# Sliding-window attention into a gated feed-forward layer: chunks 4 to 9 as units of 512 columns, with probabilities, packed sinks and ranks held elsewhere

## The chip, the cores and the metric

The kernel runs on one core of one Trainium2 chip. The metric is the device time of one execution in microseconds (us), taken from several executions; the profile is of one further execution, with its own time.

## What is computed

The reference is attention with four sink tokens and a window of 128, followed by a feed-forward layer with the activation h * tanh(softplus(h)). There are 4 batches, 8 heads, 768 positions, head size 64; then 3072 tokens of width 512 and a hidden width of 2048.

```python
scores = np.matmul(q, k.transpose(0, 1, 3, 2)) / np.sqrt(D)
keep = is_sink | ((rel >= 0) & (rel < window))
a = exp(where(keep, scores, -1e9) - max); a = a / (sum(a) + 1e-09)
x = np.matmul(a, v).transpose(0, 2, 1, 3).reshape(B * S, H * D)
h = x @ w_in
g = h * np.tanh(log1p(exp(h)))
out = g @ w_out
```

Inputs of the attention are float32, the two weight matrices float64.

## The kernel before

The tokens are worked in 12 chunks of 256 (two row tiles of 128). Chunks 0 to 3 are the first of the four batches, which see no token before them; chunks 4 to 11 are the others, sorted by batch. For each chunk, attention is done for four pairs of heads (`pair`, then `outs`) and leaves x, transposed, as a high and a low part, each exact in the format that TensorE multiplies in one pass. The feed-forward layer takes its products three times: high by high, high by low and low by high. The hidden width is cut into 16 pieces `f` of 128, or 8 pairs of pieces `f2`.

*Three forms of the feed-forward layer.* Chunks 0 to 2 are worked in turns of two `f2` each, while the weights still arrive and are split by ScalarE, VectorE and GpSimd (`weights`): `step`, narrow, products of 256 columns (L584). Chunks 3 to 9 use `step`, wide: for each piece `f` there is a result block `hp` of 2 x 256 columns, and for each of the four pieces of the inner dimension a product of 512 columns, the high weights with x's high and low part side by side (L580), and one of 256 columns, the low weights with x's high part (L581):

```python
yield nc.tensor.matmul(hp.t, wih[f].t[:, fs], xt, start=kt == 0, stop=False)
yield nc.tensor.matmul(hp.t[:, 0, :], wil[f].t[:, fs], xt[:, 0, :], start=False, stop=kt == KT - 1)
```

VectorE adds the two halves of `hp` (TENSOR_REDUCE, L590) into a block `n`. The activation follows on ScalarE and VectorE for 512 numbers at once (Exp L593, min L594, Square L595, Ln L596, Exp L597, and the product with h L598), then the copy to the high part `gh` (in the helper, L271) and the low part `gl` (in the helper, L282 to L284). The second layer is 12 products of 512 columns into two accumulators `acc` (L614). Chunks 10 and 11 together use `double`: for each piece `f`, 12 products of 512 columns, the tokens of both chunks side by side (L642), into a block that is in turn a `hp` and an `att` block, with no reduction, then the activation (Exp L645, product L650) and 12 products (L668) into four accumulators, two of tag `att` and two of tag `acc`.

*What sets the order.* Every operation is a task with a rank and one or more engines that may run it. `Plan.solve` runs through them in time with a cost for each, takes the task that can start first and among those the one of lowest rank, and so fixes the order on each engine. Blocks of SBUF and PSUM are taken by tag in the numbers of the table `TAGS`: 81 of `w`, two each of `u`, `n`, `gh`, `p2`, `sk`; in PSUM four `att`, two `hp`, two `acc`. Ranks of the feed-forward steps count through `sequence`; ranks of the attention come from `att_rank`, by a formula for chunks 3 and up. Where a plan leaves TensorE without work for some time, `emit` puts products of zeros (L786, `ZERO` columns each) there. The instructions then wait for each other by semaphores alone, as the chip runs.

*The last tile's result* leaves in two halves, one from VectorE by the queue of SP and one from ScalarE by its own queue, out of one block `w` (`store`, L687 to L694).

Of the kernel before, what the change touches and what calls it, by code (L numbers as in the profile page):

```python
# [46 lines left out]
PEN_C, PEN_S, PEN_N, PEN_J, PEN_W = 147, 0, 239, 268, 58  # L47
OTP, OVP = 1.2, 1
OTF, OVF, PACE = 1.089, 0.601, 1.542
WA, WB, WO = 1.203, -1.766, 0.423  # L50
GROUP, PART, SPARED = 3, 2, 20
PITCHN = 7
LEAD, LEADG, LEADN = 11, (54.195, 35.033, 35.128), 9
WARM, AHEAD, COLD, SPARE, ROOM = 10, 5, 2500, 250, 4
ZERO = 224
SPL = 1.5
# [187 lines left out]
class Fast(Base):  # L244
# [108 lines left out]
    def halves(self, b, j0, i0, w, pr, rank):  # L353


        nc, add = self.nc, self.plan.add
        kr, ks = Buf("raw", [P, 512, 2], I32), [Buf("w", [P, w], F32R) for _ in range(2)]
        qr, qa, qb = Buf("w", [P, 2, T]), Buf("w", [P, 2, T], F32R), Buf("w", [P, 2, T], F32R)
# [11 lines left out]
        r = rank + SPL  # L370
        k = []
        for e, z in enumerate(ks):
            a = add(r, self.copy_ways(w, lambda z=z: z.t, lambda e=e: half()[:, e, :]), ldk, [kr], [z])
            k.append(add(r + .02, self.sub_ways(w, lambda z=z: z.t[low], lambda e=e: half()[low, e, :], lambda z=z: f32(z.t[low]), more=HALF), [a], [kr, z]))
        a = add(r + .01, self.copy_ways(2 * T, lambda: qa.t, lambda: qr.t), ldq, [qr], [qa])
        q = add(r + .03, self.sub_ways(2 * T, lambda: qb.t, lambda: qr.t, lambda: f32(qa.t)), [a], [qr, qa], [qb])
        return ks, (qa, qb), [*k, q]

    def pair(self, b, c3, pr, rank, x, sk, soft):
# [6 lines left out]
        p2 = Buf("p2", [P, 6 * P])  # L386
        last, norms, sums = [], [], []
        for i in range(TB):
            r = rank + i
# [31 lines left out]
            for e in range(2):  # L421
                new = ([p2] if i == 0 else []) + ([] if soft and i else [nm, sm]) if e == 0 else []
                old = [z for z in (p2, nm, sm) if z not in new]
                j = e + 2 * i * soft
                at_ = (2 * P * i if first else 2 * WM * i) + n * e
                pv = lambda at_=at_, n=n: p2.t[:, at_:at_ + n]
# [15 lines left out]
            for e in range(2 * (not soft)):  # L442
                at_ = (2 * P * i if first else 2 * WM * i) + n * e
                row = lambda at_=at_, n=n: p2.t[:, at_:at_ + n]
# [10 lines left out]
            def tr(pt=pt, cols=cols, i=i, n=n):  # L455
                for e in range(2):
                    for x in range(2):
                        if cols[x] is not None:
                            yield nc.tensor.transpose(pt.t[:, e, x * P:(x + 1) * P], p2.t[:, 2 * P * i + n * e + cols[x]:2 * P * i + n * e + cols[x] + P], self.ident)  # L459
# [5 lines left out]
        if not first:  # L465
            pt = Buf("att", [P, 2, TB, P])

            def tr():
                for i in range(TB):
                    for e in range(2):  # L470
                        yield nc.tensor.transpose(pt.t[:, e, i, :], p2.t[:, (2 * i + e) * WM + SK:(2 * i + e + 1) * WM], self.ident)  # L471
# [8 lines left out]
            for z in (up, low):  # L480
# [5 lines left out]
                                                              lambda: p2.t[:, 0:rows].rearrange("p (i e c) -> p e i c", i=TB, e=2)[:, :, :, 0:SK]),  # L486
# [10 lines left out]
    def outs(self, first, rank, parts, x_done, sk, soft):  # L497
# [15 lines left out]
        if not first:  # L513
            ssk = Buf("att", [P, P])
            a = add(rank + OTP + 1.02, {PE: (109, lambda: nc.tensor.transpose(ssk.t, sk.t, self.ident))}, self.packs, [sk], [ssk])
# [104 lines left out]
    def double(self, sts, f, rank, begins, ends, wdeps):  # L620
# [29 lines left out]
        e = add(r + .55, {DVE: (dve_t(N), lambda: nc.vector.scalar_tensor_tensor(m.t, u.t, 1.0, hp.t, ALU.subtract, ALU.mult))}, [a], [u, hp], [m])  # L650
        gg = add(r + .57, self.copy_ways(N, lambda: gh.t, lambda: m.t), [e], [m], [gh])
        final = f == NF - 1
# [9 lines left out]
        for k, (t, part) in enumerate(((0, 0), (1, 0), (0, 1), (1, 1), (2, 0), (2, 1), (3, 0), (3, 1)) if final else order):  # L662
# [8 lines left out]
            if done:  # L671
                self.store(st, r, t, final, 2 * TB - 1)

    def store(self, st, r, t, final, last=None):
# [10 lines left out]
        ot = Buf("w" if last else "u", [P, DM])  # L685
# [3 lines left out]
        elif t == last:  # L689
            for z, (e, dma) in enumerate(((DVE, nc.sync), (ACT, nc.scalar))):  # L690
                cs = slice(z * T, (z + 1) * T)
                a = add(r + 1.7 + .1 * t, self.copy_ways(T, lambda cs=cs: ot.t[:, cs], lambda cs=cs: acc.t[:, cs], True, (e,), -1.0),
                        [st.tail], [acc] + ([ot] if z else []), [] if z else [ot])
                add(r + 1.8 + .1 * t, {SP if z == 0 else ACT: (460, lambda cs=cs, dma=dma: dma.dma_start(self.out[st.row + t * P:st.row + (t + 1) * P, cs], ot.t[:, cs]), 2500)}, [a], [ot])  # L694
# [10 lines left out]
    def sequence(self, chunks):  # L705
# [6 lines left out]
        return seq + [(n, f2) for n in range(GROUP, chunks - 2) for f2 in range(NU)] + [(chunks - 2, f) for f in range(NF)]  # L712

    def run(self):
# [8 lines left out]
        for n, (b, c3) in enumerate(chunks):  # L723
            st = SimpleNamespace(row=b * S + c3 * T, x_done=[], part={})
            if n == len(chunks) - 1:
                st.x = states[-1].x
            else:
                st.x = [[Buf("w", [P, 2, T], F32R) for _ in range(1 + (n == len(chunks) - 2))] for _ in range(KT)]
            part = n - len(chunks) + 2
            held = []  # L730
            for pr in range(NPAIR):
                if not held:
                    sk = Buf("sk", [P, P])
# [213 lines left out]
def constants(nc, top, tmp, lim):  # L947
# [18 lines left out]
    c.older, c.newer, c.elder = t([P, P], F32, "older"), t([P, P], F32, "newer"), t([P, P], F32, "elder")  # L966
# [128 lines left out]
```

## Time and profile before

| what | value |
|---|---|
| median of 3 runs | 684.61 us (684.59 to 685.14) |
| the profiled execution's own time | 686.47 us |
| its span | 684.7 us |
| granted clock of TensorE | 0.997 |
| TensorE busy | 677.2 us, 99% |
| TensorE's weight loads busy | 573.4 us, 84% |
| VectorE busy | 533.5 us, 78% |
| ScalarE busy | 536.3 us, 78% |
| GpSimd busy | 153.1 us, 22% |
| share of TensorE in the chain that ended last | 95% |

Busy time is the time in which the engine has an instruction under way; TensorE's instructions overlap, so the mean time of one in the groups is longer than the time from one start to the next, which the chain shows. A chain's row is a start, a length and what ran. The profiled execution took 1.86 us longer than the median of the runs; a difference between two kernels is worked out in the trace and taken off the median.

### The profile page before, as it was taken

What the parts mean: (1) busy time and instruction counts of PE and PEld (TensorE: products, weight loads), DVE (VectorE), ACT (ScalarE), POOL (GpSimd) and SP (SyncE); (2) the same over time, 40 slices, a digit from 0 to 9 for tenths busy, and PEclk for the clock granted to TensorE, in tenths of its full rate; (3) what the DMA queues carried; (4) which work ended last, traced back from release to release, by engine and by line L of the source; (5) the groups of instructions that cost most, each with busy time, mean ns of one, the idle gap of its engine ahead of it and who ended that gap; (6) DMA issues with size and microseconds to landing.
All of it is one profiled execution on the core that took longest, in us unless ns stands there. A gap on an engine that the chain in (4) does not pass through costs nothing.

```text
span 684.7 us, 13366 instructions
## 1 busy us (share of the span) xinstructions
PE 677.2 (99%) x4642; PEld 573.4 (84%) x4642; DVE 533.5 (78%) x1540; ACT 536.3 (78%) x1219; POOL 153.1 (22%) x144
## 2 busy tenths in 40 slices
PE   9999999999999999999999999999999999999996
PEld 5678888898888888888888888888888888888885
DVE  6998989874798988898899898888988887433333
ACT  5999999887788878777877868986886886656662
POOL 3564333411023223032222124121221210000000
PEclk9999999999999999999999999999999999999998
DMA  7555443421364145053134224234432220000001
GB/s 222 184 187 190 140 162 117 150 66 42 102 176 140 41 144 159 16 173 119 55 114 154 90 75 143 98 96 124 130 96 61 100 73 7 2 32 0 1 0 67
DMA packets 40287, 69.26 MB, mean 101 GB/s; under 512 B 4242, under 2 KB 29074, under 8 KB 40210
## 3 DMA queue, kind: packets, MB, share of 16 engines
q1 hardware_dynamic: 40064, 68.17, 31.8%
q8 instruction: 39, 0.64, 0.4%
q14 instruction: 38, 0.31, 0.1%
q10 hardware_dynamic: 146, 0.13, 0.1%
HBM read 62.00 MB, written 6.29 MB: 100 GB/s over the span
## 4 chain that ended last, share of the span: by engine, by line
PE 95%; ACT 3%; POOL 0%; DVE 0%; issue 0%; DVEq 0%; POOLq 0%
PE acc L614 31%; PE hp L580 15%; PE hp L584 9%; PE hp L581 8%; PE att L527 7%; PE att L413 5%; PE acc L668 3%; PE hp L642 3%; PE att L668 3%; PE att L642 3%; PE att L410 3%; PE att L471 2%; PE att L459 2%; ACT w L271 1%; PE att L508 1%; ACT w L313 1%
## 5 line engine op out<-in xcount | busy, mean ns | idle before, releaser
L614 PE MATMUL acc<-w,gh 128*128 128x512 f32 x640 | 166.0, 396 | 0.0
L580 PE MATMUL hp<-w,w 128*128 128x512 f32 x448 | 163.3, 400 | 0.0
L614 PEld LDWEIGHTS acc<-w,gh 128*128 128x128 f32 x640 | 113.4, 188 | 21.7 <-ACT n L271 0.2
L581 PE MATMUL hp<-w,w 128*128 128x256 f32 x448 | 125.4, 280 | 0.0
L580 PEld LDWEIGHTS hp<-w,w 128*128 128x128 f32 x448 | 84.2, 188 | 17.8 <-DVE n L590 0.3
L430 ACT ACTIVATE p<-p,nm 128x144 f32<-128x144 f32 (+2 forms) x192 | 81.0, 426 | 12.9 <-DVE nm L427 12.0
L282 POOL TENSOR_TENSOR w<-raw,w 64x416 fp32r<-64x416 f32 x41 | 44.2, 1085 | 200.3 <-ACT w L271 59.5
L614 PE MATMUL acc<-w,gl 128*128 128x512 f32 x320 | 87.1, 391 | 0.0
L581 PEld LDWEIGHTS hp<-w,w 128*128 128x128 f32 x448 | 84.5, 189 | 2.0
L590 DVE TENSOR_REDUCE n<-hp 128x256 f32<-128x512 f32 x112 | 76.7, 686 | 10.8 <-PE hp L581 9.5
L584 PE MATMUL hp<-w,w 128*128 128x256 f32 x576 | 77.6, 286 | 0.3 <-DVE u L598 0.2
L584 PEld LDWEIGHTS hp<-w,w 128*128 128x128 f32 x576 | 73.0, 191 | 4.8 <-issue 1.0
L614 PEld LDWEIGHTS acc<-w,gl 128*128 128x128 f32 x320 | 59.7, 188 | 12.8 <-issue 0.2
L271 ACT ACTIVATE gh<-n 128x512 fp32r<-128x512 f32 x69 | 43.5, 631 | 32.5 <-DVE n L598 19.4
L595 ACT ACTIVATE u<-u,bias 128x512 f32<-128x512 f32 x80 | 57.5, 719 | 11.3 <-DVE u L594 10.6
L324 POOL TENSOR_TENSOR w<-w,w 128x512 int32<-128x512 int32 x32 | 41.4, 1303 | 86.6 <-DVE w L316 29.3
L596 ACT ACTIVATE u<-u,bias 128x512 f32<-128x512 f32 x80 | 57.6, 720 | 1.3
L284 DVE TENSOR_TENSOR gl<-n,gh 128x512 fp32r<-128x512 f32 x49 | 34.3, 700 | 27.1 <-PE acc L668 24.0
L598 DVE SCALAR_TENSOR_TENSOR n<-u,n 128x512 f32<-128x512 f32 x56 | 39.7, 710 | 15.5 <-ACT u L597 15.0
L597 ACT ACTIVATE u<-u 128x512 f32<-128x512 f32 x80 | 50.1, 626 | 1.0
L593 ACT ACTIVATE u<-n 128x512 f32<-128x512 f32 x56 | 35.1, 626 | 16.6 <-DVE n L590 14.7
L527 PE MATMUL att<-pth,vq 128*64 128x64 f32 (+2 forms) x1152 | 47.8, 238 | 0.0
(135 smaller groups left out, 1227.6 us busy)
## 6 DMA issues: line engine op xcount, KB each, us to landing
vq<-v_s SPq DMA_DIRECT2D x32, 512.0 KB, 4.0
raw<-k_p SPq DMA_DIRECT2D x64, 208.0 KB, 3.5
raw<-w_in SPq DMA_DIRECT2D x16, 512.0 KB, 3.9
raw<-w_out SPq DMA_DIRECT2D x16, 512.0 KB, 3.9
w<-q_p SPq DMA_DIRECT2D x64, 128.0 KB, 3.1
y<-u SPq DMA_DIRECT2D x20, 256.0 KB, 2.0
ks<-k_p SPq DMA_DIRECT2D x16, 136.0 KB, 3.2
qh<-q_p SPq DMA_DIRECT2D x16, 128.0 KB, 3.0
```

Source lines behind the costliest of these rows:

```text
L271: ways[ACT] = act_t(n, psum) + more, lambda: nc.scalar.activation(dst(), src(), AF.Copy, scale=scale or 1.0)
L282: ways[POOL] = pool_t(n) + more, lambda: nc.gpsimd.tensor_tensor(dst(), a(), b(), ALU.subtract)
L430: a = add(r + .05 + .01 * e, {ACT: (act_t(n, ptr=2), lambda pv=pv, nm=nm, sm=sm, j=j: nc.scalar.activation(pv(), pv(), AF.Exp, bias=nm.t[: ...
L527: yield nc.tensor.matmul(o.t[e * D:(e + 1) * D, g, o0:o1], w_, pth.t[:, e, c0:c1], start=n_ == 0, stop=n_ == len(jobs) - 1)
L580: yield nc.tensor.matmul(hp.t, wih[f].t[:, fs], xt, start=kt == 0, stop=False)
L581: yield nc.tensor.matmul(hp.t[:, 0, :], wil[f].t[:, fs], xt[:, 0, :], start=False, stop=kt == KT - 1)
L584: yield nc.tensor.matmul(hp.t[:, y, :], w_.t[:, fs], xt[:, z, :], start=kt == 0 and n_ == 0, stop=kt == KT - 1 and n_ == 2)
L590: hs.append(add(r + .3 + .1 * y, {DVE: (dve_t(2 * T), lambda y=y, hp=hp: nc.vector.tensor_reduce(m.t[:, y, :], hp.t.rearrange("p z t -> p ...
L595: a = add(r + .52, {ACT: (act_t(N, ptr=1), lambda: nc.scalar.activation(u.t, u.t, AF.Square, bias=self.one))}, [a], [u])
L596: a = add(r + .53, {ACT: (act_t(N, ptr=1), lambda: nc.scalar.activation(u.t, u.t, AF.Ln, bias=self.half, scale=0.5))}, [a], [u])
L597: a = add(r + .54, {ACT: (act_t(N), lambda: nc.scalar.activation(u.t, u.t, AF.Exp, scale=-1.0))}, [a], [u])
L614: yield nc.tensor.matmul(acc[t].t, g_.t[:, y, ts_], w_.t, start=new and n_ == 0, stop=done)
```

## The change

Chunks 4 to 11 all use `double`, in four pairs; only chunk 3 stays with the wide `step` (`UNITS` = 4). In the first three doubles every first result takes a `hp` block, and the second layer is not shifted against the first (`SH` counts for the last double only). In all doubles the activation's product is written in place (`u`, not `n`). Around that:

- The probabilities of a pair are in `w` blocks (chunks 0 to 2) or a `raw` block (others) in place of tag `p2`, the packed sinks in a `ks` block in place of `sk`, q of chunks 6 and up in `n`, and results of the first three doubles in `n`; `w` has 85 blocks.
- Ranks of attention of chunks 3 and up come from the table `STARTS`, and most of the planner's constants differ; a product of zeros has 208 columns, ten at the very start become eleven.
- Two of the attention's masks are stored in 16 bits.
- The last tile's halves have a block each.

```diff
-ZERO = 224
+UNITS, PITCHP = 4, 1.737
+STARTS = {3: 11.77, 4: 18.35, 5: 23.87, 6: 33.22, 7: 39.54, 8: 48.68, 9: 55.22, 10: 65.32, 11: 72.03}
+ZERO = 208
...
-        "p2": (2, 0), "sk": (2, 0), "nm": (4, 0), "sm": (4, 0), "rc": (4, 0), "pth": (2, 0),
-        "u": (2, 0), "n": (2, 0), "gh": (2, 0), "gl": (1, 0), "w": (81, 0),
+        "nm": (4, 0), "sm": (4, 0), "rc": (4, 0), "pth": (2, 0),
+        "u": (2, 0), "n": (2, 0), "gh": (2, 0), "gl": (1, 0), "w": (85, 0),
...
-        p2 = Buf("p2", [P, 6 * P])
+        if soft:
+            p2s = [Buf("w", [P, 2 * P * (i + 1)]) for i in range(TB)]
...
+        else:
+            p2s = [Buf("raw", [P, 512, 2], I32)] * TB
...
-        eager = f >= NF - QUICK
-        r = rank - SH
+        eager = last and f >= NF - QUICK
+        r = rank - SH * last
         N = 2 * T
-        u, m = Buf("u", [P, N]), Buf("n", [P, N])
-        gh, gl = Buf("gh", [P, N], F32R), Buf("w" if f == NF - 1 else "gl", [P, N], F32R)
-        hp = Buf("att" if f % 2 else "hp", [P, N])
+        u = m = Buf("u", [P, N])
+        gh, gl = Buf("gh", [P, N], F32R), Buf("w" if last and f == NF - 1 else "gl", [P, N], F32R)
+        hp = Buf("att" if last and f % 2 else "hp", [P, N])
...
-                cs = slice(z * T, (z + 1) * T)
-                a = add(r + 1.7 + .1 * t, self.copy_ways(T, lambda cs=cs: ot.t[:, cs], lambda cs=cs: acc.t[:, cs], True, (e,), -1.0),
-                        [st.tail], [acc] + ([ot] if z else []), [] if z else [ot])
+                cs, ot = slice(z * T, (z + 1) * T), Buf("w", [P, T])
+                a = add(r + 1.7 + .1 * t, self.copy_ways(T, lambda ot=ot: ot.t, lambda cs=cs: acc.t[:, cs], True, (e,), -1.0), [st.tail], [acc], [ot])
...
-        return seq + [(n, f2) for n in range(GROUP, chunks - 2) for f2 in range(NU)] + [(chunks - 2, f) for f in range(NF)]
+        return seq + [(n, f2) for n in range(GROUP, UNITS) for f2 in range(NU)] + [(n, f) for n in range(UNITS, chunks, 2) for f in range(NF)]
...
-            if n == len(chunks) - 2:
-                self.double(states[n:], f2, r, begins, ends, wdeps)
+            if n >= UNITS:
+                self.double(states[n:n + 2], f2, r, begins, ends, wdeps, n == len(chunks) - 2)
...
-        return n * PITCHN + PITCHN / 4 * pr - LEADN + GROUP * (8 - PITCHN)
+        return STARTS[n] + PITCHP * pr
```

The new file's lines lie later by 1 from the helpers on, by 8 or 9 from `outs` on: L271 is L272 there, L580, L581 and L614 are L589, L590 and L623, L642 and L668 are L651 and L677, the products of zeros L795.

How the order moves is shown at three places. TensorE, the first layer of chunk 4, before: one block `hp`, and for each piece of the inner dimension a product of 512 and one of 256 columns (the name ahead of the arrow is the result, then x and the weights).

```order
L580 MATMUL hp_0_3431<-w_0_2987,w_0_330 128x512
L581 MATMUL hp_0_3431<-w_0_2987,w_0_368 128x256
L580 MATMUL hp_0_3431<-w_0_2989,w_0_330 128x512
L581 MATMUL hp_0_3431<-w_0_2989,w_0_368 128x256
L580 MATMUL hp_0_3431<-w_0_3303,w_0_330 128x512
L581 MATMUL hp_0_3431<-w_0_3303,w_0_368 128x256
```

The same layer after, for chunks 4 and 5 together (the first six of twelve):

```order
L651 MATMUL hp_0_3734<-w_0_2835,w_0_515 128x512
L651 MATMUL hp_0_3734<-w_0_2858,w_0_515 128x512
L651 MATMUL hp_0_3734<-w_0_2835,w_0_523 128x512
L651 MATMUL hp_0_3734<-w_0_2845,w_0_515 128x512
L651 MATMUL hp_0_3734<-w_0_2868,w_0_515 128x512
L651 MATMUL hp_0_3734<-w_0_2845,w_0_523 128x512
```

Eight rows of 512 and eight of 256 for 256 tokens and two pieces become twelve of 512 for 512 tokens and one piece. In all, the products of L580 and L581 go from 448 each to 64 each, those of L642 from 192 to 768, those of L614 from 960 to 384, those of L668 from 192 to 768, the reductions of L590 from 112 to 16, and the products of zeros of L786 from 14 to 52, of which 44 lie in the early part and 8 in chunk 3.

ScalarE, the queue ahead of the copy to the second high part `gh` of the kernel (last row; `raw` are weights as they arrive, `n` here a block of the attention), before:

```order
L313 ACTIVATE w_0_948<-raw_68 128x512
L271 ACTIVATE n_0_941<-att_0_950 128x256
L320 ACTIVATE w_0_962<-raw_68 128x512
L313 ACTIVATE w_0_971<-raw_66 128x512
L593 ACTIVATE u_0_979<-hp_0_749 128x512
L595 ACTIVATE u_0_979<-u_0_979,bias 128x512
L596 ACTIVATE u_0_979<-u_0_979,bias 128x512
L271 ACTIVATE w_0_1010<-n_0_941 128x256
L597 ACTIVATE u_0_979<-u_0_979 128x512
L271 ACTIVATE w_0_1020<-w_0_924 128x512
L593 ACTIVATE u_0_1028<-hp_0_851 128x512
L271 ACTIVATE gh_0_1038<-u_0_979 128x512
```

After, from the operation behind the same Exp on:

```order
L321 ACTIVATE w_0_995<-raw_66 128x512
L272 ACTIVATE pth_0_980<-att_0_988 128x2x256
L272 ACTIVATE n_0_1014<-rc_0_993 128x256
L272 ACTIVATE n_0_1016<-rc_0_997 128x256
L314 ACTIVATE w_0_1018<-raw_67 128x512
L272 ACTIVATE n_0_1014<-att_0_1020 128x256
L272 ACTIVATE w_0_1031<-w_0_889 128x512
L604 ACTIVATE u_0_985<-u_0_985,bias 128x512
L272 ACTIVATE w_0_1048<-n_0_1014 128x256
L605 ACTIVATE u_0_985<-u_0_985,bias 128x512
L272 ACTIVATE w_0_1060<-n_0_1016 128x256
L606 ACTIVATE u_0_985<-u_0_985 128x512
```

Between the first Exp of this result and the copy of its high part (four rows further, `gh_0_1096`) lie six operations of ScalarE in the order before and fifteen in the new one.

TensorE, chunk 3, ahead of the first transposes that have eight products of zeros in front of them, after (two rows of the eight pairs are shown):

```order
L589 MATMUL hp_0_3532<-w_0_2567,w_0_1879 128x512
L590 MATMUL hp_0_3532<-w_0_2567,w_0_1893 128x256
L795 LDWEIGHTS zero
L795 MATMUL acc_0_3108<-zero 128x208
...
L480 MATMUL att_0_3558<-ident,raw_68 128x128 x4
L623 MATMUL acc_0_3104<-w_0_1685,gh_0_3546 128x512
```

The order before has no products of zeros in chunks 3 to 11.

## Rows read from the trace of the kernel before

**Rows 1.** The page, busy time, share of the span and instructions of each engine.

```profile
PE 677.2 (99%) x4642; PEld 573.4 (84%) x4642; DVE 533.5 (78%) x1540; ACT 536.3 (78%) x1219; POOL 153.1 (22%) x144
```

**Rows 2.** Busy time by stretch (us from the start); the columns are in the first row.

```profile
core 0: us, PE busy (x) PEld busy (x) DVE busy (x) ACT busy (x) POOL busy (x), PEclk, DMA share, GB/s
...
16.00:60.00 44.00, 43.94 (x330) 31.37 (x331) 39.81 (x154) 43.39 (x140) 23.30 (x23) 1.00 0.61 194
...
190.00:590.00 400.00, 399.98 (x3021) 345.94 (x3020) 346.88 (x1048) 314.99 (x743) 90.27 (x77) 1.00 0.33 101
```

**Rows 3.** TensorE's waits: engine, tile, line, what it waited for; total us, times, longest.

```profile
PE busy L1027 <- DVE zero L1011: 1.1, 1, 1.1
PE hp L584 <- DVE u L598: 0.2, 1, 0.2
```

**Rows 4.** The chain of waits around a wide step: start, us, what.

```profile
418.30 0.44 PE att L471 x4
418.74 2.29 PE acc L614 x10
...
424.84 0.23 PE hp L580
...
427.67 0.47 PE acc L614 x2
```

**Rows 5.** The chain, the last wide steps and the first units of the double.

```profile
579.18 2.75 PE acc L614 x12
...
583.97 2.02 PE att L527 x64
585.99 0.43 PE hp L580
...
602.58 2.72 PE att L642 x12
...
608.01 2.72 PE hp L642 x12
```

**Rows 6.** The page's groups: busy us, mean ns of one, idle before.

```profile
L590 DVE TENSOR_REDUCE n<-hp 128x256 f32<-128x512 f32 x112 | 76.7, 686 | 10.8 <-PE hp L581 9.5
```

**Rows 7.** ScalarE's timeline at the second high part: start, us, what.

```profile
59.06 0.40 ACT L271 ACTIVATE w<-n 128x256 fp32r<-128x256 f32 x1
59.37 0.61 ACT L597 ACTIVATE u<-u 128x512 f32<-128x512 f32 x1
...
61.11 0.62 ACT L271 ACTIVATE gh<-u 128x512 fp32r<-128x512 f32 x1
61.63 0.62 ACT L271 ACTIVATE w<-w 128x512 fp32r<-128x512 f32 x1
62.15 0.66 ACT L313 ACTIVATE w<-raw 128x512 f32<-128x512 f32 x1
62.72 0.66 ACT L320 ACTIVATE w<-raw 128x512 int32<-128x512 uint32 x1
```

**Rows 8.** The chain at the same place.

```profile
58.42 2.16 PE hp L584 x18
...
62.35 2.75 PE acc L614 x12
```

**Rows 9.** ScalarE's waits from 16 to 60 us.

```profile
ACT n L271 <- PE att L508: 1.0, 1, 1.0
ACT u L595 <- DVE u L594: 0.5, 1, 0.5
```

**Rows 10.** The timeline of the last tile's two halves.

```profile
678.77 0.42 DVE L273 TENSOR_SCALAR w<-acc 128x256 f32<-128x256 f32 x1 [0.67 <-PE acc L668]
...
679.23 0.38 ACT L271 ACTIVATE w<-acc 128x256 f32<-128x256 f32 x1 [0.54 <-DVE w L273]
```

**Rows 11.** ScalarE's timeline, one activation of a wide step, first and last step.

```profile
433.94 0.61 ACT L593 ACTIVATE u<-n 128x512 f32<-128x512 f32 x1
...
438.44 0.63 ACT L271 ACTIVATE gh<-n 128x512 fp32r<-128x512 f32 x1
```

More of the change, by code (lines that the diff above doesn't have):

```diff
@@ L385, in pair @@
         pth = Buf("pth", [P, 2, 2 * T])
-        p2 = Buf("p2", [P, 6 * P])
+        if soft:
+            p2s = [Buf("w", [P, 2 * P * (i + 1)]) for i in range(TB)]
+            for z in p2s:
+                z.brief = True
+        else:
+            p2s = [Buf("raw", [P, 512, 2], I32)] * TB
+        flat = (lambda z: z.t) if soft else (lambda z: f32(z.t.rearrange("p n t -> p (n t)")))
         last, norms, sums = [], [], []
         for i in range(TB):
-            r = rank + i
+            r, p2 = rank + i, p2s[i]
+            base = 0 if soft else 2 * P * i if first else 2 * WM * i
             if not (soft and i):
@@ L442, in pair @@
             for e in range(2 * (not soft)):
-                at_ = (2 * P * i if first else 2 * WM * i) + n * e
-                row = lambda at_=at_, n=n: p2.t[:, at_:at_ + n]
+                at_ = base + n * e
+                row = lambda at_=at_, n=n, p2=p2: flat(p2)[:, at_:at_ + n]
                 norm.append(add(r + .09 + .01 * e, {
@@ L514, in outs @@
             ssk = Buf("att", [P, P])
-            a = add(rank + OTP + 1.02, {PE: (109, lambda: nc.tensor.transpose(ssk.t, sk.t, self.ident))}, self.packs, [sk], [ssk])
+            a = add(rank + OTP + 1.02, {PE: (109, lambda: nc.tensor.transpose(ssk.t, sk.t[:, 0:P], self.ident))}, self.packs, [sk], [ssk])
             self.packs = []
@@ L618, in step, with double @@
                 self.store(st, r, t, f2 == NF // 2 - 1)
-    def double(self, sts, f, rank, begins, ends, wdeps):
+    def double(self, sts, f, rank, begins, ends, wdeps, last):
         nc, add = self.nc, self.plan.add
@@ L649, in double @@
         a = add(r + .54, {ACT: (act_t(N), lambda: nc.scalar.activation(u.t, u.t, AF.Exp, scale=-1.0))}, [a], [u])
-        e = add(r + .55, {DVE: (dve_t(N), lambda: nc.vector.scalar_tensor_tensor(m.t, u.t, 1.0, hp.t, ALU.subtract, ALU.mult))}, [a], [u, hp], [m])
+        e = add(r + .55, {DVE: (dve_t(N), lambda: nc.vector.scalar_tensor_tensor(m.t, u.t, 1.0, hp.t, ALU.subtract, ALU.mult))}, [a], [u, hp])
         gg = add(r + .57, self.copy_ways(N, lambda: gh.t, lambda: m.t), [e], [m], [gh])
-        final = f == NF - 1
+        final = last and f == NF - 1
         gk = []
@@ L671, in double, with store @@
             if done:
-                self.store(st, r, t, final, 2 * TB - 1)
-    def store(self, st, r, t, final, last=None):
+                self.store(st, r, t, True, last and t == 2 * TB - 1, "w" if last else "n")
+    def store(self, st, r, t, final, halves=False, tag="u"):
         nc, add, acc = self.nc, self.plan.add, st.acc[t]
@@ L684, in store @@
             return
-        ot = Buf("w" if last else "u", [P, DM])
+        ot = Buf(tag, [P, DM]) if not halves else None
         if old:
@@ L688, in store @@
                 ot.t, acc.t, -1.0, old.t, ALU.mult, ALU.subtract))}, [st.tail], [acc, old], [ot])
-        elif t == last:
+        elif halves:
             for z, (e, dma) in enumerate(((DVE, nc.sync), (ACT, nc.scalar))):
-                cs = slice(z * T, (z + 1) * T)
-                a = add(r + 1.7 + .1 * t, self.copy_ways(T, lambda cs=cs: ot.t[:, cs], lambda cs=cs: acc.t[:, cs], True, (e,), -1.0),
-                        [st.tail], [acc] + ([ot] if z else []), [] if z else [ot])
-                add(r + 1.8 + .1 * t, {SP if z == 0 else ACT: (460, lambda cs=cs, dma=dma: dma.dma_start(self.out[st.row + t * P:st.row + (t + 1) * P, cs], ot.t[:, cs]), 2500)}, [a], [ot])
+                cs, ot = slice(z * T, (z + 1) * T), Buf("w", [P, T])
+                a = add(r + 1.7 + .1 * t, self.copy_ways(T, lambda ot=ot: ot.t, lambda cs=cs: acc.t[:, cs], True, (e,), -1.0), [st.tail], [acc], [ot])
+                add(r + 1.8 + .1 * t, {SP if z == 0 else ACT: (460, lambda cs=cs, dma=dma, ot=ot: dma.dma_start(self.out[st.row + t * P:st.row + (t + 1) * P, cs], ot.t), 2500)}, [a], [ot])
             return
@@ L724, in run @@
             st = SimpleNamespace(row=b * S + c3 * T, x_done=[], part={})
-            if n == len(chunks) - 1:
+            part = (n - UNITS) % 2 if n >= UNITS else -1
+            self.calm = n >= UNITS + 2
+            if part == 1:
                 st.x = states[-1].x
             else:
-                st.x = [[Buf("w", [P, 2, T], F32R) for _ in range(1 + (n == len(chunks) - 2))] for _ in range(KT)]
-            part = n - len(chunks) + 2
+                st.x = [[Buf("w", [P, 2, T], F32R) for _ in range(2 + part)] for _ in range(KT)]
             held = []
```

38 lines of the change are left out of this document (19 added, 19 removed).

## The prediction

> **What bounds the kernel now.** I read the page's busy times first. TensorE is busy 677.2 of the 684.7 us of the profiled execution's span, VectorE 533.5, ScalarE 536.3 [rows 1]: one engine is full, two have a fifth of their time free. The table of stretches says where that holds [rows 2]: from 190 to 590 us, where chunks 3 to 9 run, TensorE is busy 399.98 of 400 us, with VectorE at 347 and ScalarE at 315. From 16 to 60 us it is different: ScalarE is busy 43.39 of 44 us beside a busy TensorE, so there both are full, and part of TensorE's work is multiplications of zeros that the plan puts where it expects a wait. The list of TensorE's waits holds two entries of 1.1 and 0.2 us [rows 3]; no wait of chunks 4 to 9 is in it. So in the middle the time is the sum of TensorE's instructions, and an edit there is worth what it does to that sum. At the start it is worth what it does to ScalarE.
>
> **The stream of chunks 4 to 9.** The order shows that the first layer's 384 pairs (512 columns, then 256) of these six chunks become 576 instructions of 512 columns. The columns are the same: 384 x 768 = 576 x 512 = 294,912. The second layer keeps its 576 instructions. So only the time per column can differ, and the trace has both forms without a pause. The chain of waits gives the pairs: eight of them run from 424.84 to 427.67 us [rows 4], 2.83 us, 353.8 ns a pair; twelve of the second layer behind such pairs take 2.75 us [rows 5]. One of a chunk's eight steps (8 pairs and 12) is thus 5.58 us. The last two chunks already run in the new form: 12 first-layer instructions take 2.72 us, 226.7 ns each, and the next twelve of the same kind start 5.43 us after the first [rows 5]. Both hold 24 x 512 columns' worth: 8 x 768 + 12 x 512 = 12,288. The clean difference is 0.15 us, and there are 6 x 8 = 48 such units: **7.2 us less**.
>
> That is the most. What the trace of before never shows is the new form with attention inside it. The order puts 84 bursts of attention between instructions of 512 columns in the three new doubles. After a short burst ten second-layer instructions took 2.29 us, 229 ns each instead of 226.7 [rows 4], which is 0.03 us per twelve; after the long burst of 64 the first product took 0.43 instead of 0.23 us [rows 5], but those bursts, as many as before, cost that in either form. I take 84 x 0.03 = 2.5 us back, and as the other end twice that, 5.0. The term is **-4.7**, between -7.2 and -2.2.
>
> A rule speaks against this term, and stands by itself: the Trainium skill, TensorE: Matmul & The Clock Gate, section Back-to-back issue gap, gives an isolated matmul N/2.4 + 2.5 ns, by which the first layer's 192 fewer instructions would save 192 x 2.5 ns, 0.5 us as an estimate, where the pairs give 384 x 13.7 ns, 5.3; it puts a pair at 325 ns, and the trace does not agree (353.8 [rows 4]).
>
> **VectorE.** 96 of the 112 reductions that add a pair's two halves go (each 686 ns [rows 6]): 66 us of VectorE. With TensorE busy 399.98 of 400 us no instruction of it waited for them [rows 2, 3], so I cost this at nothing. It only loosens the chain of the activation, below. Probabilities in the blocks of other tags, packed sinks and q in other tags, and the masks in half the width change buffers, not the count of TensorE's instructions; nothing as long as the buffers come free in time, which is what the second rival is about.
>
> **Eight products of zeros.** In the last wide steps of chunk 3 the new order has eight in a row ahead of the transposes of the first new attention. They are 208 columns; at 226.7 ns for 512 that is 0.092 us each, **+0.8** together. Below, 0.7; above, 1.5, if what they stand for lasts longer than they do.
>
> **The start.** Here ScalarE's order counts. In before the copy that makes the second result's high part starts at 61.11 and ends at 61.73 us, and TensorE, which has worked without a break, uses it at 62.35 [rows 7, 8]. In the new order 130 operations of ScalarE's queue end with that copy instead of 123, and 293 products of TensorE lie ahead of its use instead of 287. What is added ahead: three copies of 256, five of 512 in place of four of 256, one more of 512 and one more of each unpacking of weights. By the starts in ScalarE's timeline, 0.31, 0.52 and 0.57 us from one to the next [rows 7]: 3 x 0.31 + 5 x 0.52 - 4 x 0.31 + 0.52 + 2 x 0.57 = 3.95 us. TensorE's six more products take six times 0.12 (18 in 2.16 us [rows 8]), 0.7. So the copy comes 3.2 us later against TensorE than it did. Of that 0.5 is the margin that it had (62.35 less 61.73 less a hand-over of some 0.1), and 1.0 is a pause of ScalarE for TensorE ahead of it [rows 9], which the fuller queue covers: **+1.7**. Below, the second pause (0.5) goes too, and the wide copies turn out cheaper by 0.7: +0.5. Above, nothing is won back: +3.2. The number of zero products in the early part speaks for a cost too: 44 instead of 14, so 30 more at 0.092, 2.8 us, if each took time in which there was work. In before such a product mostly filled a wait, hence not my value.
>
> **The end.** The last tile's ScalarE half waits 0.54 us for VectorE's half of the same block [rows 10]; with a block for each half both start together, save some 0.1 for the hand-over: **-0.4**. Below nothing, above -0.5.
>
> The sum: -4.7 + 0.8 + 1.7 - 0.4 = **-2.6 us**. The profiled execution took 686.47 us with a span of 684.7; the runs' median is 684.61. I take the difference off the median: **682.0 us**.
>
> **Rivals.** *The start eats the gain.* ScalarE is full until 60 us [rows 2], so what its order adds there is paid in full: +3.2 and 1.5 for the zeros of chunk 3, against -4.7 and -0.4: 684.2. For it: 44 early products of zeros show that the plan itself saw waits there. Against: ScalarE's operations are moved ahead, not added, and TensorE's order has other work of attention that could come in between. Chance 0.22.
>
> *Too few blocks in the new doubles: slower.* In before one double runs alone at the end and uses attention's blocks for every second unit. The new three run beside attention, with two blocks for first results, and their four accumulators take two of attention's four. Attention then waits for blocks, and so do ScalarE's and VectorE's operations behind it in order. Each unit's activation chain, from the first exponential at 433.94 to the end of the high part at 439.07, took 5.1 us in before [rows 11]; the new order gives it 12 + 12 products at least, 5.43 us [rows 5], plus whatever attention lies between: by count of its products, at these rows' spacings, some ten units have 6.0 to 6.6 us, the median about 7.9. It decides when the chain with its hand-overs passes those 6.6 us. If 20 units then wait 0.3 us, that is 6 us: 688.0. For it: both engines work in order, so an operation of attention that waits for a block holds up the chain behind it. Against: the chain has lost both reductions. Chance 0.13. The Trainium skill, Perfetto Trace Analysis, section Optimization Strategy, reads an even row of gaps on the full engine as too little SBUF or PSUM for the next tile; no row of before shows such gaps.
>
> *The pair's extra time isn't the pair's.* A pair costs 13.7 ns more than one and a half of 512. If that belonged to running beside attention and not to the form, it would stay, and only the second layer's 2.75 to 2.72 remains, 0.03 x 48 = 1.4: 684.6 - 1.4 + 1.7 + 0.8 - 0.4 = 685.3. The Trainium skill's rule above (TensorE: Matmul & The Clock Gate, Back-to-back issue gap) would come out near this. The row speaks against it: the eight pairs of [rows 4] stand with no attention between them. Chance 0.05.
>
> *Everything comes in*: -7.2 in the stream and the start at its lower end: 684.6 - 7.2 - 0.4 + 0.5 + 0.8 = 678.3; with half of that extra, 680. Chance 0.15. That the change doesn't do what it says is excluded by the order.
>
> **How the numbers follow.** The forecast, 682.0, has 0.45; half-way to either end of its largest term, 1.2 us, it reaches from 680.8 to 683.2. A measurement of this kernel can tell about 0.2% from no change, 1.4 us. Faster (below 683.2): forecast and the full gain, 0.45 + 0.15 = 0.60. Within: the first and third rivals, 0.22 + 0.05 = 0.27. Slower: 0.13. The range leaves out the slower rival's 0.13 above and the last third of the full gain, 0.05, below: **678.8 to 686.0**.
>
> **What would show it.** In the profile of after, 12 first-layer products in the chain at 2.72 us with attention near, and 2.72 to 2.75 for twelve of the second layer; VectorE's busy time lower by 60 to 70 us; TensorE without a break from 190 on. The chain's use of the second high part some 1.7 us later than TensorE's work alone would have it, with an entry of the waits on ScalarE by 62 us. Wrong would be: entries of the second layer waiting for the high part, again and again, in chunks 4 to 9 (the slower rival), or 12 products at 2.8 us and more (the third), or a start that is no later at all.

## The result and the profile after

The changed kernel takes 689.75 us (median of 4 executions, 688.85 to 691.1) where the kernel before takes 684.76 on the same chip; the ratio on record is 1.0066, 95% interval 1.0049 to 1.0082. It is slower by about 5 us; 682.0 was forecast, and the range ended at 686.0.

One thing about the profiled executions comes first. That of before, on which the forecast rests, had a span of 684.7 us; a second profile of the unchanged kernel (e1 below) has 683.1, and its runs the old median. So the trace of before is 1.6 us longer than e1's, and after's (687.5; its run 0.5 below the median) is an ordinary one. I compare with e1 where it matters.

One line of after's page, the table of stretches (columns as in [rows 2]) and two of the four entries of TensorE's waits:

```profile
PE 677.8 (99%) x4489; PEld 564.0 (82%) x4489; DVE 487.7 (71%) x1475; ACT 532.7 (77%) x1206; POOL 135.0 (20%) x126
```

```profile
16.00:60.00 44.00, 43.87 (x339) 31.61 (x336) 39.62 (x151) 43.89 (x141) 23.80 (x22) 1.00 0.61 191
...
190.00:590.00 400.00, 398.58 (x2772) 334.52 (x2772) 294.63 (x947) 310.64 (x718) 67.61 (x57) 1.00 0.32 97
```

```profile
PE hp L589 <- DVE u L607: 0.6, 1, 0.6
PE hp L651 <- DVE u L659: 0.5, 2, 0.3
```

VectorE's busy time fell from 533.5 [rows 1] to 487.7, by 46 us and not by the 66 of the reductions alone: other work came to it (GpSimd has 18 us less than before, 135.0 for 153.1). TensorE, 99% busy, shows 1.4 us of idle time between 190 and 590 where before had 0.02 [rows 2]. None of this shows 5 us: a product that starts late behind the one before still counts as busy, and so do the products of zeros.

So I add up spacing. For each kernel the sum runs over all products, from one start to the next, less a clean time: 226.7 ns for 512 columns [rows 5] and in proportion for fewer in both layers, fixed values for attention's products (124.5 ns for 272 columns, 109 for a transpose; the same in all kernels), nothing for products of zeros. The rest is **time lost**, in us, by stretch of the execution. Its level depends on the values chosen for attention, and differences of 0.2 mean nothing:

| kernel | to 60 us | 60 to 180 | 180 to 260 | 260 to 600 | after 600 | sum |
|---|---|---|---|---|---|---|
| before, the trace of the rows | 13.1 | 5.0 | 2.1 | 8.9 | 6.1 | 35.2 |
| before, e1 | 11.3 | 5.1 | 2.2 | 8.8 | 6.2 | 33.7 |
| after | 13.3 | 5.7 | 4.2 | 7.8 | 7.1 | 38.1 |
| after, e2 | 14.1 | 6.0 | 3.8 | 8.0 | 7.1 | 39.0 |

Against e1 after loses 2.0 at the start, 0.6 behind it, 2.0 around chunk 3 and 0.9 at the end, and wins 1.1 where the new doubles run: 4.4 in all, which is the difference of the spans (687.5 - 683.1).

### The profile page after: what moved, and what is told of

Read it like the earlier page. It is cut to its first block, busy times and chain, and to the rows that moved or that the text cites. A ratio compares the mean times of both kernels' runs of the same rounds, so it can differ in the third digit from the quotient of the medians.

```text
span 687.5 us, 13052 instructions
## 1 busy us (share of the span) xinstructions
PE 677.8 (99%) x4489; PEld 564.0 (82%) x4489; DVE 487.7 (71%) x1475; ACT 532.7 (77%) x1206; POOL 135.0 (20%) x126
## 4 chain that ended last, share of the span: by engine, by line
PE 86%; ACT 5%; DVE 4%; DMA 2%; issue 1%; SPq 1%; POOL 0%; DVEq 0%; ACTq 0%; POOLq 0%
PE hp L651 20%; PE att L677 12%; PE acc L677 11%; PE acc L623 11%; PE hp L593 9%; PE att L536 6%; PE att L421 4%; PE att L651 3%; PE hp L589 2%; PE att L418 2%; PE att L468 2%; PE att L480 2%; DMA raw<-k_p 2%; PE hp L590 1%; DVE w L285 1%; DMA raw<-w_in 1%
## 5 line engine op out<-in xcount | busy, mean ns | idle before, releaser
L651 PE MATMUL hp<-w,w 128*128 128x512 f32 x672 | 168.8, 394 | 0.5 <-DVE u L659 0.5
L651 PEld LDWEIGHTS hp<-w,w 128*128 128x128 f32 x672 | 123.5, 188 | 26.0 <-DVE u L659 1.0
L272 ACT ACTIVATE gh<-u 128x512 fp32r<-128x512 f32 x85 | 53.4, 629 | 34.6 <-DVE u L659 29.4
L285 DVE TENSOR_TENSOR gl<-u,gh 128x512 fp32r<-128x512 f32 x71 | 53.6, 755 | 36.6 <-PE acc L677 23.6
L593 PE MATMUL hp<-w,w 128*128 128x256 f32 x576 | 78.4, 286 | 0.2
L593 PEld LDWEIGHTS hp<-w,w 128*128 128x128 f32 x576 | 72.9, 190 | 4.5 <-DVE u L607 1.1
L677 PE MATMUL att<-w,gh 128*128 128x512 f32 x256 | 70.7, 396 | 0.0
L677 PE MATMUL acc<-w,gh 128*128 128x512 f32 x256 | 69.7, 391 | 0.0
L623 PE MATMUL acc<-w,gh 128*128 128x512 f32 x256 | 66.2, 396 | 0.0
L438 ACT ACTIVATE raw<-raw,nm 128x144 f32<-128x144 f32 (+2 forms) x144 | 59.0, 410 | 9.3 <-DVE nm L435 8.7
L654 ACT ACTIVATE u<-hp 128x512 f32<-128x512 f32 x56 | 33.3, 595 | 31.4 <-PE hp L651 30.1
L659 DVE SCALAR_TENSOR_TENSOR u<-u,hp 128x512 f32<-128x512 f32 x56 | 38.4, 685 | 26.7 <-ACT u L658 26.1
L677 PEld LDWEIGHTS acc<-w,gh 128*128 128x128 f32 x256 | 47.7, 188 | 10.1
L677 PEld LDWEIGHTS att<-w,gh 128*128 128x128 f32 x256 | 46.4, 188 | 9.3
L623 PEld LDWEIGHTS acc<-w,gh 128*128 128x128 f32 x256 | 45.6, 188 | 8.5 <-issue 0.3
L536 PEld LDWEIGHTS att<-pth,vq 128*64 128x64 f32 x1152 | 38.9, 138 | 10.5 <-issue 3.8
```

The lines of the kernel that those rows point to most:

```text
L272: ways[ACT] = act_t(n, psum) + more, lambda: nc.scalar.activation(dst(), src(), AF.Copy, scale=scale or 1.0)
L285: way = dve_t(n) + more, lambda: nc.vector.tensor_tensor(dst(), a(), b(), ALU.subtract)
L438: a = add(r + .05 + .01 * e, {ACT: (act_t(n, ptr=2), lambda pv=pv, nm=nm, sm=sm, j=j: nc.scalar.activation(pv(), pv(), AF.Exp, bias=nm.t[: ...
L536: yield nc.tensor.matmul(o.t[e * D:(e + 1) * D, g, o0:o1], w_, pth.t[:, e, c0:c1], start=n_ == 0, stop=n_ == len(jobs) - 1)
L593: yield nc.tensor.matmul(hp.t[:, y, :], w_.t[:, fs], xt[:, z, :], start=kt == 0 and n_ == 0, stop=kt == KT - 1 and n_ == 2)
L623: yield nc.tensor.matmul(acc[t].t, g_.t[:, y, ts_], w_.t, start=new and n_ == 0, stop=done)
```

## The experiments

**e1 and e2: both kernels again**, unchanged. (The theories of a run are those of its expectation.)

> The kernel before, unchanged, once more. Theory 1 (the change costs about 5 us in every execution): the same time as before within 0.1%, a span near 683 us, and TensorE's time over the clean rates (226.7 ns for 512 columns) about 33 us, so 2 us less than in the profiled execution of before, which took 686.47. Theory 2 (executions of before themselves differ by 2 us from one to the next): a span near 684.7 again, and a spread of the runs of 1 us or more.

> The kernel after, unchanged, once more. Theory 1 (TensorE waits at the same places in every execution): the pauses of 0.5, 0.3, 0.3, 0.4 us between 380 and 428 us and the one of 0.8 us at 199 us stand at the same instructions, and the time is 688.8 to 691.1 again. Theory 2 (what is lost there hangs on when loads land): other pauses, at other places, with the sum differing by 1 us or more.

e1: 685.14 us beside 685.27 for before on that chip, span 683.1, 33.7 us lost: theory 1, though one run of ten reaches 686.7. e2: 689.6. The four pauses in the doubles stand at the same products, later by 0.8 to 0.9 us, and that at 199 us too: theory 1 there. The four in after's timeline:

```profile
379.66 0.67 PE L421 MATMUL att<-w,w 128*128 128x272 f32 x4
...
379.92 0.68 DVE L659 SCALAR_TENSOR_TENSOR u<-u,hp 128x512 f32<-128x512 f32 x1
...
380.66 1.19 PE L651 MATMUL hp<-w,w 128*128 128x512 f32 x4 [0.33 <-DVE u L659]
```

```profile
427.64 0.66 PE L421 MATMUL att<-w,w 128*128 128x272 f32 x4
427.78 0.69 DVE L659 SCALAR_TENSOR_TENSOR u<-u,hp 128x512 f32<-128x512 f32 x1 [1.05 <-ACT u L658]
...
428.52 1.66 PE L651 MATMUL hp<-w,w 128*128 128x512 f32 x6 [0.21 <-DVE u L659]
```

```profile
404.47 1.54 PE L651 MATMUL hp<-w,w 128*128 128x512 f32 x6
406.14 2.08 PE L536 MATMUL att<-pth,vq 128*64 128x64 f32 x64
...
411.51 1.55 PE L651 MATMUL hp<-w,w 128*128 128x512 f32 x6
413.20 0.63 PE L480 MATMUL att<-ident,raw 128*128 128x128 f32 x4
```

At 380.66 and 428.52 a first layer waits until VectorE's product with h has read the `hp` block of the unit two earlier: with two blocks the ring is short. At 406.14 and 413.20 it is attention that waits, a burst of its second products and one of transposes, each behind six first-layer products. By spacing the four cost 0.5, 0.3, 0.3 and 0.4 us in order of time, 1.5 together, of which 0.9 are for `hp` blocks.

What e2 adds is the start. The wait of ScalarE for the first weights was 0.76 us in after, here 1.80:

```profile
11.18 0.68 ACT L314 ACTIVATE w<-raw 128x512 f32<-128x512 f32 x1 [1.80 <-SPq L1100]
```

ScalarE works in order, so all behind it came 1.0 us later, and the span is 0.9 longer.

**e3: after without the new doubles.**

```diff
-UNITS, PITCHP = 4, 1.737
+UNITS, PITCHP = 10, 1.737
```

> All of after except the new doubles: chunks 4 to 9 are wide steps again, 384 pairs of 512 and 256 columns, q in w blocks; tags, ranks, the start, masks and tail as in after. Theory 1 (the doubles still give something, 1.5 us by the trace, and the start, chunk 3 and the tail lose it): slower than after by 1 to 3 us, 691 to 693. Theory 2 (the doubles themselves are what makes it slow, by their waits and by recovery after each burst): faster than after by 2 us or more, 687 or less. 16 products of zeros that stand ahead of the last double here (1.4 us) come on top in both.

692.26 us, 2.7 slower than after on the same chip (e2); 16 products of zeros ahead of the last double, 1.44 us in its chain, are in it. Theory 1: the doubles by themselves are worth some 1 us, 1.2 by these medians, though only 0.6 by the spans of the two profiles (689.6 and 687.5, e3's from its fastest run). To 180 us it loses what after loses (13.4 and 5.8), so that loss is not theirs.

**e4: bursts where no attention runs.** The last double of before gets a burst ahead of each first layer.

```diff
+                for j in range(4 * (kh == 0)):
+                    if f % 2:
+                        yield nc.tensor.transpose(hp.t[:, 0:P], f32(woh[f].t[:, j * P:(j + 1) * P]), self.ident)
+                    else:
+                        yield nc.tensor.matmul(hp.t[:, 0:272], woh[f].t[:, j * P:(j + 1) * P], woh[f].t[:, 0:272], start=True, stop=True)
```

> The kernel before, with a burst of TensorE's own work ahead of each first layer of the last double, where no attention runs: four products of 272 columns in even units, four transposes of 128 in odd ones, into the block that the first layer then overwrites. Theory 1 (a burst by itself slows the next ten or so products of 512 columns, whatever the other engines do): behind each burst the spacing is 228 to 236 ns for ten products, then 226.7; 0.05 to 0.1 us lost a burst beside its own 0.50 or 0.44 us, in all 16 x 0.47 + 16 x 0.07 = 8.6 us more than before. Theory 2 (the slow products near attention come from the other engines' attention work): 226.7 ns from the first product on, and 7.5 us more.

693.13 us in one run, 7.9 above before; span 691.4, 8.3 above e1's. The chain (L642 and L640 are bursts there):

```profile
620.15 0.50 PE hp L642 x4
620.65 2.75 PE hp L647 x12
...
626.12 0.44 PE att L640 x4
626.56 2.77 PE att L647 x12
```

The twelve products behind a burst take 2.75 to 2.77 us instead of 2.72 [rows 5]: 0.03 to 0.05 a burst, without any attention. Theory 1 by its pattern (229 to 235 ns in the first seven or so, then 226.7), at the lower end of its size or just below it.

**e5, e12: products of zeros.** e5 leaves out all but those of the first 4 us, e12 only the eight of chunk 3 (`t.start < 100000`).

```diff
-... / ((n / 1.2) if early else n / 2.4 + 2.5) + 1)):
+... / ((n / 1.2) if early else n / 2.4 + 2.5) + 1) * (t.start < 4000)):
```

> After without its products of zeros, but for those of the first 4 us. Theory 1 (they stand in time in which TensorE could have worked): faster by up to 41 x 0.092 = 3.8 us, of which 0.7 lie in chunk 3: about 686. Theory 2 (they only fill waits that are there anyway): the same within 0.2%, with the pauses open in the list of waits, if the granted clock stays at 0.99 or more.

> After without the eight products of zeros in chunk 3; all others stay. Theory 1 (they delay TensorE by their own time): 0.7 us less over the clean rates between 240 and 260 us, and the kernel faster by 0.7 us, near 688.9. Theory 2 (they fill a wait for the first transposes behind them): the same, with a wait of 0.7 us of these transposes in the trace.

e5: 690.06 us, no faster by its median, and the granted clock 0.995. That speaks for theory 2, but weakly: its four runs spread from 687.81 to 691.11, and in its profile the first weights came another 1.0 us later than in e2 (ScalarE began to unpack at 12.19 us). e12: 689.36; the time can't tell 0.4 us, the trace can. Chain of after, then of e12:

```profile
250.29 0.73 PE acc L795 x8
251.02 0.44 PE att L480 x4
```

```profile
250.32 0.23 PE hp L589
250.56 0.12 PE hp L590
250.68 0.44 PE att L480 x4
```

Without the eight the transposes follow the first layer at once: they filled no wait and cost their 0.73 us.

**e6: the old tail**, in after.

```diff
-                cs, ot = slice(z * T, (z + 1) * T), Buf("w", [P, T])
+                cs = slice(z * T, (z + 1) * T)
+                ot = Buf("w", [P, DM]) if z == 0 else ot
...
```

> After with the last tile's two halves in one block again, so VectorE's half first and ScalarE's behind it, out by ScalarE's queue last. Theory 1 (the order of the halves and the queue of the last store make the tail 0.7 us longer than before's): from the start of the last product to the end of the span 6.3 us instead of 7.1, and the kernel faster by 0.7 us. Theory 2 (landing times vary): 7 us as in after, no difference.

688.76 us (1.0053, 1.0036 to 1.007): the intervals overlap, and after 600 us it loses 6.8 against 7.1. Inconclusive for the 0.7. That the new blocks brought nothing is plain in after's timeline:

```profile
681.26 0.38 ACTq L702 DMA_DIRECT2D y<-w  x1
681.26 0.42 DVE L274 TENSOR_SCALAR w<-acc 128x256 f32<-128x256 f32 x1 [1.10 <-ACT w L272]
681.71 0.33 SPq L702 DMA_DIRECT2D y<-w  x1
```

VectorE's half now waits for ScalarE's, as ScalarE's did for VectorE's [rows 10]: the one block that both still use is `acc`, and their waits keep them one behind the other. That `acc` is the reason was not tried. The last product starts at 680.42 us, the last store 1.29 later, as in before (678.35 and 679.64).

**e7, e13, e14: constants and blocks.** e7 is after with the constants of the first chunks as in before; e14 before with those of after; e13 after's blocks with before's constants, starts and wide steps. The edit of e14, in part (the others are its reverse, e13 with `UNITS` 10 and the starts by the old rule `7 * n - 6`):

```diff
...
-OTF, OVF, PACE = 1.089, 0.601, 1.542
-WA, WB, WO = 1.203, -1.766, 0.423
+OTF, OVF, PACE = 1.094, 0.475, 2.396
+WA, WB, WO = 1.164, -1.263, 0.410
...
-LEAD, LEADG, LEADN = 11, (54.195, 35.033, 35.128), 9
+LEAD, LEADG, LEADN = 11, (74.498, 31.443, 30.477), 9
...
```

> After with the planner's constants for the first chunks as in before (penalties, offsets of the attention's steps, pace, weights, lead; the table of starts of chunks 3 to 11 stays). Theory 1 (the order on ScalarE and VectorE in the first 60 us loses 2.5 us against before): TensorE's time over the clean rates at 60 us is near 11.3 instead of 13.3 to 14.1 and the kernel faster by 2 us or more, 687.5 or less. Theory 2 (it is the probabilities in w blocks that hold up the start, whatever the constants): 13 us or more over the clean rates at 60 us, and no gain.

> All blocks and tags of after (probabilities in w and raw blocks, packed sinks in ks, 85 w, 16-bit masks, tail), with the planner's constants, the starts of attention and the wide steps of before. Theory 1 (the constants of after, not its blocks, lose the 2 to 2.8 us by 60 us): 11.3 to 11.6 over the clean rates at 60 us, as in e1 and e11; later on up to 6 us lost between 60 and 180 us, as in e8, because chunk 3 and the weights share raw blocks. Theory 2 (the blocks lose it): 13 or more at 60 us.

> Before with the planner's constants of after for the first chunks (penalties, offsets, pace, weights, lead, one more product of zeros ahead), and the blocks, the starts of chunks 3 to 11 and the wide steps of before. Theory 1 (the constants lose it): 13 or more over the clean rates at 60 us, and slower than before by 1.5 us or more. Theory 2 (the blocks lose it): 11.3 to 11.6 at 60 us and 685 us.

**e8, e11: one kind of block alone**, in before: probabilities of chunks 3 and up in `raw` (e8), and those of chunks 0 to 2 in `w` (e11). The first lines of e8's edit:

```diff
-        p2 = Buf("p2", [P, 6 * P])
+        p2 = Buf("p2", [P, 6 * P]) if soft else Buf("raw", [P, 512, 2], I32)
...
```

> Before with one part of the change alone: the probabilities of chunks 3 and up in raw blocks, which the weights and the k loads use too. Theory 1 (the shared blocks make loads late, as the chain of after shows at 187 to 199 us: a load of k, then VectorE, then TensorE): slower than before by 1 us or more, with a load of raw in the chain. Theory 2 (the three raw blocks are enough): the same as before within 0.2%.

> Before with one part of the change alone: the probabilities of chunks 0 to 2 in w blocks, those of the other chunks in their own tag as before. Theory 1 (these blocks are what loses 2 us and more by 60 us, whatever the constants): TensorE's time over the clean rates at 60 us 13 or more, against 11.3 in e1, and the kernel slower by 1.5 us or more, 686.5 and up. Theory 2 (other tags or the moved attention do that): 11.3 at 60 us, and 685 us as before.

**e9, e10: starts.** e9 holds the loads of k and q of chunks 4 and up back (`z.ready` = 24000 in `halves`); e10 is e3 with the starts of before (`STARTS = {n: 7.0 * n - 6 ...}`).

> After with one thing held back: the loads of q and k of chunks 4 and up are planned no earlier than 24 us, so that no load of q of chunk 4 is issued at 7.2 us, between the first weights (issued at 4.6) and the first batch's own k and q. Theory 1 (that load makes the first weights land late, at 10.1, 11.2 or 12.2 us in three executions of after's start, against 10.2 and 10.3 in before, and ScalarE, in order, holds everything behind its unpacking): the unpacking starts at 10.2 or earlier, the runs spread by less than 1 us, and the median is 1 us lower, 688.6 or less. Theory 2 (the landing varies by itself): 10.1 to 12.2 still, and no gain.

> As e3 (after with wide steps in chunks 4 to 9), and the starts of the attention of chunks 3 to 11 by the rule of before, later by 3 to 5 ranks at chunks 3 to 5; blocks and tags as in after. Theory 1 (the doubles need the attention of chunk 4 and 5 early, and this work, moved ahead into the stretch where ScalarE is full, is what chunk 3 and the start lose): TensorE's time over the clean rates from 60 to 250 us falls from e3's 9.1 to about 7.4 as in before, and the time to 687 to 688. Theory 2 (the blocks are the cause, probabilities in w and raw blocks, whatever the starts): still 9 us over the clean rates there, 690 or more.

These seven beside e1, e3 and after, with the time lost, and the number of products of zeros that the plan puts between 60 and 180 us:

| kernel | median us | to 60 us | 60 to 180 | 180 to 260 | 260 to 600 | after 600 | zeros, 60 to 180 |
|---|---|---|---|---|---|---|---|
| e1, before | 685.14 | 11.3 | 5.1 | 2.2 | 8.8 | 6.2 | 0 |
| e11, `w` blocks | 686.43 | 12.6 | 5.0 | 2.2 | 8.6 | 6.5 | 0 |
| e8, `raw` blocks | 691.25 | 10.8 | 11.1 | 2.8 | 8.8 | 6.9 | 29 |
| e13, all blocks | 692.16 | 11.5 | 9.6 | 2.4 | 9.0 | 7.9 | 19 |
| e14, constants | 690.92 | 12.0 | 8.3 | 2.5 | 9.8 | 6.6 | 29 |
| e10, blocks and constants | 692.05 | 13.5 | 9.5 | 2.1 | 9.2 | 6.9 | 26 |
| e3, and the new starts | 692.26 | 13.4 | 5.8 | 3.4 | 9.0 | 8.6 | 6 |
| after, and the doubles | 689.75 | 13.3 | 5.7 | 4.2 | 7.8 | 7.1 | 6 |
| e7, after with old constants | 694.51 | 13.8 | 8.0 | 4.1 | 9.8 | 7.1 | 8 |
| e9, after with later loads | 691.69 | 13.2 | 8.3 | 3.6 | 7.5 | 7.0 | 21 |

*To 60 us.* The `w` blocks of the first chunks alone lose 1.3 us there and nothing between 60 and 600 (e11): near theory 1, which asked for 13 and 686.5. (The expectation of e13 counts e11 among the kernels that lose 11.3 to 11.6; its trace doesn't bear that out.) In e11 the plan has 11 more products of zeros there; the first row is e1's, the second e11's, with the ten ahead of the kernel's first work in both counts:

```profile
0.00:60.00 60.00, 5.46 (x24) 2.65 (x24) 0.15 (x1) 1.00 0.66 208
0.00:60.00 60.00, 6.85 (x35) 3.64 (x35) 0.15 (x1) 1.00 0.65 205
```

But with all the blocks of after only 0.2 are lost by 60 us (e13: theory 1's figure), with the constants alone 0.7 (e14: neither theory), and with both 2.2 (e10). With the old constants after is no better there (e7, 13.8: theory 2) and 4.8 us slower as a whole. So the 2.0 us of after are not the sum of its parts, and no one part was shown to make them.

*From 60 to 180 us.* The blocks without the rest lose 4.5 us there (e13), the `raw` blocks alone 6.0 (e8). e8's trace has TensorE waiting there, which e1's has not:

```profile
PE hp L585 <- DVE u L599: 2.3, 3, 0.9
```

Most of the rest is 29 products of zeros, which the plan puts where it leaves TensorE without other work. But e14, which has none of the new blocks, has as many and loses 3.2 us there, and is 5.8 us slower than before. The products of zeros, in e8 and in e14:

```profile
60.00:180.00 120.00, 3.46 (x29) 2.55 (x29) 0.00 (x0) 1.00 0.30 99
60.00:180.00 120.00, 3.46 (x29) 2.55 (x29) 0.00 (x0) 1.00 0.35 115
```

So this loss is not one of the blocks alone: either part, put into the plan of before without the other, makes a plan with such holes, and so do both without the new starts (e10); how much of e8's loss constants chosen for its blocks would win back was not tried. e8's theory 1 has the size, but not the cause that it names: no load stands in its chain between 30 and 185 us. With the new starts the loss goes (e10 to e3, 9.5 to 5.8), at 1.3 us more between 180 and 260 and 1.7 at the end, and the time stays the same. e10 gave theory 2.

e9's first weights came at 10.0 us, as its theory 1 said, but its plan lost 2.6 us more than after's behind 60 us, and its runs spread from 690.86 to 693.12; that the early load of q makes the first weights late was not shown by it. In after that load stands in SP's queue ahead of k:

```profile
7.24 0.72 SPq L298 DMA_DIRECT2D w<-q_p  x1
8.15 0.54 SPq L298 DMA_DIRECT2D ks<-k_p  x1
```

The loss at chunk 3 has a chain of its own in after:

```profile
187.44 4.64 DMA raw<-k_p
...
192.62 0.56 ACT w L272 x2
193.18 3.15 DMA raw<-k_p
196.42 0.48 DVE raw L454 x2
196.93 1.09 DVE w L285 x2
198.06 0.69 DVE w L285
198.98 0.61 DVE u L607
199.63 0.50 PE hp L589
```

The second load goes out when ScalarE has copied the k before it. SP's queue, too, shows two issues of such loads, the second of them this one, as one stretch of 4.98 us:

```profile
188.80 4.98 SPq L298 DMA_DIRECT2D raw<-k_p  x2
```

k of the next attention comes late into `raw`, VectorE splits it ahead of the product with h, and TensorE's next first layer waits 0.6 us for that product's block, 0.8 by spacing. With the 0.73 of the eight zeros that is 1.5 of the 2.0 lost there. e10, with the same blocks and later starts, has no such pause and loses 2.1 in that stretch, as before does.

## Why the prediction was wrong

Summed up by time lost, the trace of after is 4.4 us longer than e1's where 2.6 shorter was forecast. Of these 7.0 us the stream has 3.6, the end 1.3, chunk 3 1.2, the stretch from 60 to 180 us 0.6 and the start 0.3.

- **The stream (-4.7, between -7.2 and -2.2): -1.1 by the table, -0.6 to -1.2 by e3.** The clean rates held: TensorE's chain of after has 12 products in 2.72 us with attention around, and the pairs' own excess, 6.0 us in e1 (380 pairs from 246 us on, 16 ns over the clean rate each; some 1.5 us of it is the time of transposes and long bursts booked on the pair behind them), is gone. The step that failed is "84 x 0.03 = 2.5 us back": it was 4.5, with 1.5 of pauses that the term had at nothing.

```profile
267.53 2.72 PE hp L651 x12
270.25 0.50 PE att L421 x4
270.75 1.39 PE hp L651 x6
...
294.39 1.42 PE hp L651 x6
```

  Six products behind a burst take 1.39 to 1.42 us where clean ones take 1.36: 0.03 to 0.06 in the first six alone, and some ten are slow. Over after's 85 runs of 512 columns the excess is 7.9 us without pauses; 26 follow transposes, whose time is in part booked on the next product (28 + 313 ns instead of 109 + 227), and 11 follow the long burst (0.11 us, as before); less these 3.4 it is 4.5, or 0.05 a burst, against 0.03 to 0.05 in the quiet double (e4). That lies inside the 5.0 that the prediction took as its other end. The pairs of before hardly show a burst (behind four products of 272 columns the first is 10 ns over the clean rate, not more than others). And 1.5 us of pauses came on top, 0.9 of them for a `hp` block.
- **The start (+1.7, between +0.5 and +3.2): +2.0 by 60 us, +2.8 in e2.** The second high part starts 2.7 us later than in e1 (62.15 for 59.44) with 0.7 us more of TensorE's products ahead: 2.0 net. The size came out, but partly by luck: the sum had 3.2 - 0.5 - 1.0, and the pause of 1.0 us [rows 9] isn't in e1's trace at all, where ScalarE waits 0.5 us in that stretch. It belonged to the one execution that the rows are from. TensorE did not wait at that place, as I had asked for; it came late as well. What came behind 60 us (+0.6) I had not counted, and the experiments don't show what in the change makes the 2.0.
- **The eight zeros (+0.8): 0.73**, as said. But chunk 3 loses 2.0, with 0.8 for the late k behind the early starts: the rest was in no term, only in "nothing as long as the buffers come free in time".
- **The end (-0.4): +0.9.** With a block of SBUF for each half the two halves still went one behind the other, so nothing was won. Most of the 0.9 is the landing of the last store: 5.8 us from its issue in after and e2, 5.1 in before and e1 (but 5.9 in e8, which has the old tail, so its cause is open).
- **VectorE at nothing** was right as a price: 46 us less (60 to 70 were expected), and nothing shows TensorE faster for it.
- The rule of the Trainium skill (TensorE: Matmul & The Clock Gate, Back-to-back issue gap) gives 0.5 us for the merged products, an estimate from its 2.5 ns a matmul; the pairs' excess that went is some 4.5 us without what was only booked on them, so the trace does not bear it out.
- **The second rival** (too few blocks, 688.0, chance 0.13) had the sign. Its place, first layers waiting for a `hp` block, is in the trace, at two units and not at 20, with 0.9 of the 5 us. Its reason came in elsewhere too: the late k at chunk 3 waits for a `raw` block, of which the probabilities now take some.

Open is what makes the 2.0 us of the start, since neither the blocks nor the constants alone do, and what lets the landing of the first weights differ by 2 us (10.1 to 12.2). The doubles with the old blocks were not tried. None of the runs is faster than before.

## What to carry to other kernels

Price a wider instruction by what it does behind an interruption, and not by its clean stretch alone: here 4.5 of a 7 us gain went into some ten slightly slow products behind each of 84 bursts. Where a change needs room, list what gives it up, and for each of those blocks which loads and which engine's queue now wait for it; here a load of k that waits for its block is part of the 2.0 us lost at chunk 3. A part of a planned kernel that is tried alone is tried in a plan whose constants were chosen without it: the new constants alone cost 5.8 us here, more than the whole change. And take the sum of terms in a second profile of the same kernel, if its first is off its own median.

## What the runs showed of the hardware that I had not expected

After four short products (272 columns or transposes) TensorE needs about eight products of 512 columns to come back from 231 to 226.7 ns, with no attention running (e4). The first weights, issued at 4.6 us in every execution, let ScalarE start at 9.6 to 10.5 us in most kernels, but at 11.2 and 12.2 in two executions of after's start.
